# A gated linear attention and a four-expert block on one core: the last two groups of tokens share each expert's weights, and the attention state is stored in 96 columns

## The chip, the cores and the metric

The kernel runs on one core of a Trainium2 chip. The metric is the device time of one launch in microseconds; the kernel before the change takes 1087.85 us (median of 3 runs, 1086.94 to 1088.24). The engines are named as the profile names them: PE is the matrix engine (PEld its weight loads), DVE the vector engine, ACT the scalar engine, POOL the general engine, SP the engine that issues most of the transfers.

## What is computed

A recurrent attention with a decay for each key dimension comes first. Its output, 3072 tokens of 384 features, goes through four experts of two layers each, whose results are added with normalized weights.

```python
# B, H, S, D = 4, 8, 768, 48
for t in range(S):
    state = alpha[:, :, t, :, None] * state + einsum('bhd,bhe->bhde', k[:, :, t], v[:, :, t])
    y[:, :, t] = einsum('bhd,bhde->bhe', q[:, :, t], state)
x = y.transpose(0, 2, 1, 3).reshape(3072, 384)
# E, F = 4, 1024
p = domain_probs / (domain_probs.sum(-1, keepdims=True) + 1e-09)
for e in range(E):
    out += p[:, e:e + 1] * (maximum(x @ w1[e], 0.0) @ w2[e])
```

All data are float32.

## The kernel before

**Units and groups.** The sequence is cut into 6 blocks of 128 steps; a block of one batch is a *unit*, so there are 24. Attention makes 128 tokens of x from a unit. The experts work on groups of units: group 0 has 2, groups 1 to 5 have 4 each (512 tokens), and group 6, the last, has 2 (256 tokens). A group goes through all four experts before the next begins, with an `up` (first layer) and a `down` (second layer) for each.

**Two ways to multiply.** A float32 product is either done *whole*, [...] (two matmul records in the trace), or *in parts*: both factors are split into parts that fit the faster `float32r` type, and three matmuls give the product. Splitting the weights is done once, in groups 0 and 1, and the parts are kept in DRAM; splitting x and the hidden activations costs work on ACT and DVE.

```python
split1 = lambda gi, e, c=0: gi > 0 and (gi < len(groups) - 1 or c < NQ - 1)   # first layer
split2 = lambda gi, e, c=0: 1 < gi < len(groups) - 1                          # second layer
```

So before the change group 6 runs its first layer in parts for three of the four weight pieces (a piece is a quarter of F, two of the eight `fc` tiles), and the fourth piece and its whole second layer as whole float32.

**The first layer**, for one tile `fc` of 128 hidden features (PSUM tiles with the tag "g" come from a ring of four):

```python
one = ps.tile([P, NT], F32, name="one", tag="g", bufs=4)[:, :hi - lo]
...
two = ps.tile([P, NT], F32, name="two", tag="g", bufs=4)[:, :n]
for out, terms in ((one, (1, 0)), (two, (2,))):
    for part in terms:
        for kc in range(KC):
            nc.tensor.matmul(out, lhsT=w[:, part, kc], rhs=xTs[gi][:, part, kc, :n], ...)
while finish:                       # the rest of the tile before
    for _ in finish.popleft(): pass
t = work.tile([P, NT], F32, name="t")[:, :n]
nc.scalar.activation(out=t, in_=one, func=ACT.Copy, scale=FINE)
if split2(gi, e):
    nc.vector.tensor_add(t, t, two)
    finish.append(hidden_parts(t, parts))
else:
    nc.vector.tensor_add(whole, t, two)
    finish.append(rectified(whole))
...
def hidden_parts(x, parts):
    top, low, dif = parts
    nc.scalar.activation(out=top, in_=x, func=ACT.Relu, scale=TRIM)
    yield
    nc.vector.scalar_tensor_tensor(out=low, in0=x, scalar=0.0, in1=top.bitcast(F32),
                                   op0=ALU.max, op1=ALU.subtract)
    n = x.shape[-1]
    make_dif(*(part[:, :n // 2] for part in parts))      # one more DVE operation, half the columns
    later.append([part[:, n // 2:] for part in parts])   # the other half, done during down
```

**The second layer** takes two units at a time where it is in parts (four PSUM tiles), one unit at a time where it is whole (one PSUM tile). Each result is added into the accumulator of its unit:

```python
nc.vector.scalar_tensor_tensor(out=acc, in0=part, scalar=scale, in1=acc,
                               op0=ALU.mult, op1=ALU.add)
```

**Attention** runs in the background. Each unit is a generator of 17 steps (`BEATS`); `deal()` gives every step a moment on a clock that counts the matmuls of the experts, and `advance()` emits the steps that are due between those matmuls. Two units are under way at a time. The x of a group is finished before the second layer of the last expert of the group before, where `split_x` splits it. The parts of a unit that the change touches:

```python
st = sts[b]                                      # [P, NP=4, 2, HD=64]: two heads of a pair, 64 columns each
yps = ps.tile([P, KC, P], F32, name="yps", tag="w")
for c in range(KC):                              # KC = 3
    if c < 2:
        turns = [[(j, 2 * c + j // 2, j % 2, slice(0, QUAD)) for j in range(4)]]      # QUAD = 32
    else:
        turns = [[(p, p, i, slice(QUAD, HD)) for p in range(NP)] for i in range(2)]
    terms = [(t, past) for past in ((True, False) if cb > 0 else (False,)) for t in turns]
    for n, (turn, past) in enumerate(terms):
        for j, p, i, cols in turn:
            nc.tensor.matmul(yps[QUAD * j:QUAD * (j + 1), c, :],
                             lhsT=st[:, p, i, cols] if past else rv[:, 2 * p + i, cols],
                             rhs=QT[:, p, :] if past else lat[:, 2 * p + i, :], ...)
...
sps = ps.tile([P, NP, 2, HD], F32, name="sps", tag="w")
for p in range(NP):                              # 128 x 128 products, the new part of the state
    nc.tensor.matmul(sps[:, p], lhsT=KB[:, p, :], rhs=rv[:, 2 * p:2 * p + 2, :], start=True, stop=True)
```

`past` is what the state of the earlier blocks adds; the 20 units with cb > 0 have it.

Of the kernel before, what the change touches and what calls it, by code (L numbers as in the profile page):

```python
# [20 lines left out]
def kernel(  # L21
# [41 lines left out]
    P = 128  # L63
# [40 lines left out]
    lat = const.tile([P, H, P], F32, name="lat")  # L104
    sts = [const.tile([P, NP, 2, HD], F32, name=f"st{b}") for b in range(B)]

# [3 lines left out]
    half = B // 2  # L110
    groups = [order[:half]] + [order[i:i + B] for i in range(half, len(order), B)]
    units = [u for g in groups for u in g]
    place = {u: (gi, i) for gi, g in enumerate(groups) for i, u in enumerate(g)}
# [33 lines left out]


    split1 = lambda gi, e, c=0: gi > 0 and (gi < len(groups) - 1 or c < NQ - 1)
    split2 = lambda gi, e, c=0: 1 < gi < len(groups) - 1  # L150
    makes = [lambda gi, e: gi == 0, lambda gi, e: gi == 1]


    def load(u, names):
        if u >= len(units):
            return
        cb, b = units[u]
        for nm in names:
            src = srcs[nm][b, :, cb * P:(cb + 1) * P, :].rearrange("h s d -> s h d")
            if nm != "v":  # L160
                nc.sync.dma_start(out=raw(u, nm)[:, :, :D], in_=src)
                continue

            pairs = raw(u, nm).rearrange("p (a i) d -> p a i d", i=2)
            src = src.rearrange("p (a i) d -> p a i d", i=2)
            nc.sync.dma_start(out=pairs[:, :, 0, :D], in_=src[:, :, 0])
            nc.sync.dma_start(out=pairs[:, :, 1, :QUAD], in_=src[:, :, 1, :QUAD])
            nc.sync.dma_start(out=pairs[:, :, 1, D:], in_=src[:, :, 1, QUAD:])

# [3 lines left out]
            for l in range(2)]  # L173
    wt = ({}, {})

    AHEAD = 4
# [4 lines left out]
    def load_piece(l, i, beside=False):  # L181
        if i >= E * NQ * len(groups):
            return
        gi, k = divmod(i, E * NQ)
        e, c = divmod(k, NQ)
        if (split1, split2)[l](gi, e, c):
            w = wt[l][i] = wts.tile([P, 3, KC * QF], F32R, name=f"w{l + 1}",
                                    bufs=AHEAD if l == 0 else NQ)
            nc.sync.dma_start(out=w.bitcast(F32), in_=kept[l][k])
            return  # L190
# [72 lines left out]
    def attention(u):  # L263
# [139 lines left out]

        st = sts[b]
        yps = ps.tile([P, KC, P], F32, name="yps", tag="w")
        for c in range(KC):

            if c < 2:
                turns = [[(j, 2 * c + j // 2, j % 2, slice(0, QUAD)) for j in range(4)]]
            else:  # L410
                turns = [[(p, p, i, slice(QUAD, HD)) for p in range(NP)] for i in range(2)]
            terms = [(t, past) for past in ((True, False) if cb > 0 else (False,)) for t in turns]
            for n, (turn, past) in enumerate(terms):
                for j, p, i, cols in turn:
                    nc.tensor.matmul(  # L415
                        yps[QUAD * j:QUAD * (j + 1), c, :],
                        lhsT=st[:, p, i, cols] if past else rv[:, 2 * p + i, cols],
                        rhs=QT[:, p, :] if past else lat[:, 2 * p + i, :],
                        start=(n == 0), stop=(n == len(terms) - 1))
        gi, slot = place[cb, b]  # L420
        if slot == 0:
            if gi == 0:
                xTs[gi] = work.tile([P, 3, KC, NT], F32R, name="xT", bufs=1)
                xraws[gi] = xTs[gi][:, 2].bitcast(F32)
            else:
                xraws[gi] = work.tile([P, KC, NT], F32, name="x_raw", bufs=1)
        nc.scalar.copy(out=xraws[gi][:, :, slot * P:(slot + 1) * P], in_=yps)
        yield

        if cb < NCB - 1:  # L430
            KB = AT
            nc.scalar.copy(out=KB, in_=turned(lambda p: KT[:, p, :]))
            yield
            sps = ps.tile([P, NP, 2, HD], F32, name="sps", tag="w")
            for p in range(NP):
                nc.tensor.matmul(sps[:, p], lhsT=KB[:, p, :], rhs=rv[:, 2 * p:2 * p + 2, :],  # L436
                                 start=True, stop=True)
            for i in range(2):
                rows = slice(HD * i, HD * (i + 1))
                old, add = st[rows, :, i, :], sps[rows, :, i, :]  # L440
                if cb == 0:
                    nc.vector.tensor_copy(out=old, in_=add)
                else:
                    nc.vector.tensor_mul(old, old, decs[-1][rows].broadcast_to([HD, NP, HD]))
                    nc.vector.tensor_add(old, old, add)

        load(u + 2, "v")
        yield

    def split_x(gi, step):  # L450

        n = len(groups[gi]) * P
        if step == 0:
            xTs[gi] = work.tile([P, 3, KC, NT], F32R, name="xT", bufs=1)
            for kc in range(KC):
                nc.scalar.activation(out=xTs[gi][:, 0, kc, :n], in_=xraws[gi][:, kc, :n],
                                     func=ACT.Copy, scale=TRIM)
        else:
            kc = step - 1
            split_rest(xraws[gi][:, kc, :n], [xTs[gi][:, part, kc, :n] for part in range(3)])  # L460


    def up(gi, e, fc, slots=None):
# [3 lines left out]
        c, f = divmod(fc, FPQ)  # L467
        i = (gi * E + e) * NQ + c
        if fc == 0 and begins:
# [12 lines left out]
        col = slice(f * P, (f + 1) * P)  # L482
        if split1(gi, e, c):
            w = wt[0][i].rearrange("p t (c f) -> p t c f", f=QF)[:, :, :, col]
# [4 lines left out]
        one = ps.tile([P, NT], F32, name="one", tag="g", bufs=4)[:, :hi - lo]  # L489
        if not split1(gi, e, c):  # L490
            for kc in range(KC):
# [3 lines left out]
        else:  # L495
            two = ps.tile([P, NT], F32, name="two", tag="g", bufs=4)[:, :n]
            for out, terms in ((one, (1, 0)), (two, (2,))):
                for part in terms:
                    for kc in range(KC):
                        nc.tensor.matmul(out, lhsT=w[:, part, kc], rhs=xTs[gi][:, part, kc, :n],  # L500
                                         start=(part == terms[0] and kc == 0),
# [16 lines left out]
        if f == FPQ - 1 and ends:  # L518
            if gi > 0:
                del wt[0][i]  # L520
                load_piece(0, i + AHEAD)
            elif i == E * NQ - 1:
                for k in range(AHEAD):
                    load_piece(0, i + 1 + k)
            while late:
# [23 lines left out]
    def down(gi, e, slots, between):  # L549


        first = (gi * E + e) * NQ
        halves_ = split2(gi, e)
# [32 lines left out]
        background()  # L586
        if slots[-1] == len(groups[gi]) - 1:
            while makes[1](gi, e) and (making or splitting):
                background()

            for c in range(NQ):
                del wt[1][first + c]
                if c < NQ // 2:
                    load_piece(1, first + NQ + c)
# [3 lines left out]
    def add_up(gi, e, slot, kind, part):  # L598
# [3 lines left out]
        if e == 0 and (kind == 0 or not split2(gi, e)):  # L602
            accs[cb, b] = hid.tile([P, DM], F32, name="acc", bufs=B)
        acc = accs[cb, b]
# [8 lines left out]
        if e == E - 1:  # L613
            del accs[cb, b]
            row = b * S + cb * P
            stores.append(lambda: (nc.sync if gi == len(groups) - 1 else nc.gpsimd).dma_start(
                out=out[row:row + P, :], in_=acc))
# [9 lines left out]
    def deal():  # L627
# [6 lines left out]
        t = 0.0  # L634
        for gi in range(len(groups)):
            for e in range(E):
                part = 1 - 1 / len(groups[0]) if gi == e == 0 else 1
                t += cost(0, gi, e) * FCH * part
                if e == E - 1:
                    wanted.append(t)  # L640
                t += cost(1, gi, e) * len(groups[gi]) * part
        for gi in range(1, len(groups)):
            n = len(groups[gi])
            first = wanted[gi - 1] if gi > 1 else 0.0
            space = (wanted[gi] - MARGIN - first) / (n if gi > 1 else (n + 1) / 2)
            if gi == 1:
                space /= 2
            for k in range(n):
                u = sum(map(len, groups[:gi])) + k
                end = wanted[gi] - MARGIN - (n - 1 - k) * space  # L650
                begin = max(end - 2 * space, ends[-2])
# [11 lines left out]
    with tc.manual_schedule():  # L663
# [47 lines left out]

        for gi, e in ((gi, e) for gi in range(len(groups)) for e in range(E)):
            rest = gi == e == 0
# [5 lines left out]
            for k, slots in enumerate(turns):  # L719

                between = deque()
                if e == E - 1 and gi + 1 < len(groups):
                    for step, at in enumerate((0.0, 0.52, 0.62, 0.72)):
                        at = at * len(turns) - k
                        if 0 <= at < 1:
                            between.append((at, lambda step=step: split_x(gi + 1, step)))
                down(gi, e, slots, between)
                if gi == len(groups) - 1 and e == E - 1:
                    stores.popleft()()
        while stores:  # L730
# [29 lines left out]
```

## Time and profile before

| | from the page or the trace |
|---|---|
| time | 1087.85 us (profiled execution: span 1085.3 us) |
| busy share of PE, DVE, ACT, POOL | 98%, 69%, 52%, 3% |
| clock granted to PE | full but for short spells (0.998 in the mean) |
| chain that ended last | PE 87%, ACT 5%, DVE 5% |
| up and down of one expert of group 4, with attention between | 696.8 to 719.3 us and 719.3 to 739.3 us |
| up and down of the last expert of group 5, no attention left | 970.9 to 987.4 us and 987.4 to 1004.4 us |
| group 6, from its first matmul to the last | 1004.4 to 1081.7 us |
| transfers | 273.68 MB, 252 GB/s in the mean |

The page gives busy time of each engine, the span in 40 slices, the chain of work that ended last, and groups of instructions with the mean duration of one. [...] the pace of a row of matmuls is read from start to start in the timeline, not from that mean. A line in the timeline merges neighbours of one kind: start, length, engine, line, and how many.

### The profile page before, as it was taken

The page shows a single profiled execution, that of the slowest core. Times are in us where ns is not written, and L with a number is a line of the kernel's source. Part 1 is how long each engine was busy: PE and PEld are TensorE (multiplying, and loading weights), DVE is VectorE, ACT ScalarE, POOL GpSimd, SP SyncE. Part 2 cuts the span into 40 slices and gives each one's busy share as a digit, 9 for nine tenths or more (in the row PEclk, how much of TensorE's full clock was granted, in tenths as well). Part 3 has the DMA queues.
Part 4 walks back from the last instruction along what each step waited for, and adds up shares of the span by engine and source line. Part 5 has one row for each costly group of instructions (what it writes and reads, how often), then busy time and mean ns, then how long its engine had stood idle before and what let it go on. Part 6 is the DMA issues. An engine that isn't in the chain of part 4 may idle for free.

```text
span 1085.3 us, 21700 instructions
## 1 busy us (share of the span) xinstructions
PE 1062.9 (98%) x8532; PEld 892.9 (82%) x8532; DVE 747.7 (69%) x1625; ACT 560.7 (52%) x1191; POOL 35.3 (3%) x75
## 2 busy tenths in 40 slices
PE   8889899999999999999999999999999999999998
PEld 8767677686776798898898898898988998899876
DVE  5588678647557869778878787986786876757111
ACT  5787776674646555545546445555454454222321
POOL 2000000000000100000000000000000000000000
PEclk9999999999999999999999999999999999999999
DMA  8597789786696967657759559477477568545982
GB/s 124 154 327 216 228 266 370 290 312 234 211 322 218 400 203 275 273 169 301 254 171 358 201 190 357 158 276 306 151 291 287 201 259 349 235 197 238 309 312 91
DMA packets 166197, 273.68 MB, mean 252 GB/s; under 512 B 120624, under 2 KB 140976, under 8 KB 142032
## 3 DMA queue, kind: packets, MB, share of 16 engines
q1 hardware_dynamic: 156704, 230.06, 61.0%
q0 software_dynamic: 6016, 42.08, 9.9%
q8 instruction: 67, 1.10, 0.4%
q10 hardware_dynamic: 3376, 0.17, 0.3%
q14 instruction: 34, 0.28, 0.1%
HBM read 229.81 MB, written 42.47 MB: 251 GB/s over the span
## 4 chain that ended last, share of the span: by engine, by line
PE 87%; ACT 5%; DVE 5%; issue 2%; POOL 0%; ACTq 0%; DVEq 0%; POOLq 0%
PE ops L576 24%; PE one L500 21%; PE ops L580 13%; PE two L500 10%; PE sc L328 6%; PE yps L415 4%; PE one L492 3%; PE tp L260 3%; ACT qb L302 2%; PE sps L436 1%; PE far L383 1%; PE idle L689 1%; DVE near L338 1%; DVE hT L534 1%; DVE t L509 1%
## 5 line engine op out<-in xcount | busy, mean ns | idle before, releaser
L576 PE MATMUL ops<-w,hT 128*128 128x384 f32 x1536 | 284.7, 340 | 2.1 <-DVE acc L609 2.1
L500 PE MATMUL one<-xT,w 128*128 128x512 f32 (+1 forms) x1104 | 275.3, 385 | 0.8 <-DVE xT L242 0.8
L576 PEld LDWEIGHTS ops<-w,hT 128*128 128x128 f32 x1536 | 265.9, 188 | 5.7 <-DVE acc L609 2.8
L500 PEld LDWEIGHTS one<-xT,w 128*128 128x128 f32 x1104 | 194.5, 188 | 43.4 <-issue 2.6
L507 ACT ACTIVATE t<-one 128x512 f32<-128x512 f32 (+1 forms) x184 | 103.1, 560 | 149.4 <-PE one L500 148.8
L580 PE MATMUL ops<-hT 128*128 128x384 f32 x512 | 176.1, 491 | 0.0
L302 ACT COPY qb<-QT 64x256 f32<-64x256 f32 x336 | 136.5, 406 | 70.1 <-DVE QT L283 40.2
L500 PE MATMUL two<-xT,w 128*128 128x512 f32 (+1 forms) x552 | 148.3, 377 | 0.0
L580 PEld LDWEIGHTS ops<-hT 128*128 128x128 f32 x512 | 94.0, 191 | 56.5 <-issue 1.3
L534 DVE SCALAR_TENSOR_TENSOR hT<-t,hT 128x512 fp32r<-128x512 f32 x128 | 88.7, 693 | 61.1 <-ACT hT L532 59.7
L532 ACT ACTIVATE hT<-t 128x512 fp32r<-128x512 f32 x128 | 80.9, 632 | 95.8 <-DVE t L509 94.6
L500 PEld LDWEIGHTS two<-xT,w 128*128 128x128 f32 x552 | 100.3, 188 | 19.8
L542 DVE SCALAR_TENSOR_TENSOR hT<-hT 128x256 fp32r<-128x256 f32 x256 | 101.3, 421 | 4.4
L509 DVE TENSOR_TENSOR t<-t,two 128x512 f32<-128x512 f32 x128 | 87.3, 682 | 20.6 <-PE two L500 12.6
L609 DVE SCALAR_TENSOR_TENSOR acc<-ops,p_all,acc 128x384 f32<-128x384 f32 x88 | 53.3, 612 | 58.6 <-PE ops L580 42.3
L338 DVE COPY_PREDICATED near<-masks,sc 128x256 f32<-128x256 uint8 x144 | 77.0, 535 | 17.6 <-PE sc L328 14.5
L309 DVE TENSOR_TENSOR QT<-QT,dec 128x256 f32<-128x256 f32 x144 | 60.7, 421 | 32.5 <-ACT qb L302 32.0
L328 PEld LDWEIGHTS sc<-qb,KT 128*64 128x64 f32 x2304 | 72.5, 138 | 8.9 <-issue 6.3
L512 DVE TENSOR_TENSOR hT<-t,two 128x512 f32<-128x512 f32 (+1 forms) x56 | 32.1, 574 | 65.8 <-ACT t L507 56.1
L328 PE MATMUL sc<-qb,KT 128*64 128x64 f32 x2304 | 76.7, 223 | 0.3 <-ACT qb L302 0.3
L321 DVE TENSOR_TENSOR KT<-KT,dec 128x256 f32<-128x256 f32 x144 | 60.1, 417 | 2.2 <-PE tp L260 2.2
L320 ACT COPY KT<-KT 128x256 f32<-128x256 f32 x144 | 59.8, 415 | 3.1
(79 smaller groups left out, 927.0 us busy)
## 6 DMA issues: line engine op xcount, KB each, us to landing
w<-kept SPq DMA_DIRECT2D x156, 1152.0 KB
kept<-w POOLq DMA_DIRECT2D x32, 1152.0 KB, 7.5
hT<-in_moe_w_dram SPq DMA_DIRECT2D x48, 384.0 KB
w<-in_moe_w_dram SPq DMA_DIRECT2D x60, 128.0 KB
ra<-in_alpha_dram SPq DMA_DIRECT2D x23, 192.0 KB
rk<-in_k_dram SPq DMA_DIRECT2D x23, 192.0 KB
rq<-in_q_dram SPq DMA_DIRECT2D x23, 192.0 KB
out_dram<-acc POOLq DMA_DIRECT2D x22, 192.0 KB, 5.8
```

The costliest lines, as they stand in the source:

```text
L302: nc.scalar.copy(out=qb[rows, :, i, :].rearrange("p a (b r) -> p a b r", r=m), in_=qv[rows])
L309: nc.vector.tensor_mul(qv, qv, spread(dv[:, :, :, 0], m))
L328: nc.tensor.matmul(out[HALF * s:HALF * (s + 1), 2 * p:2 * p + 2, :], lhsT=KTs[li][:, p, HALF * s:HALF * (s + 1)], rhs=qbs[li][:, p, :, QUA ...
L338: nc.vector.copy_predicated(near.rearrange("p a (b two r) -> p a b two r", two=2, r=m)[:, :, :, 1, :], mk.unsqueeze(1).broadcast_to([P, H, ...
L500: nc.tensor.matmul(out, lhsT=w[:, part, kc], rhs=xTs[gi][:, part, kc, :n], start=(part == terms[0] and kc == 0), stop=(part == terms[-1] a ...
L507: nc.scalar.activation(out=t, in_=one, func=ACT.Copy, scale=FINE)
L509: nc.vector.tensor_add(t, t, two)
L532: nc.scalar.activation(out=top, in_=x, func=ACT.Relu, scale=TRIM)
L534: nc.vector.scalar_tensor_tensor(out=low, in0=x, scalar=0.0, in1=top.bitcast(F32), op0=ALU.max, op1=ALU.subtract)
L542: nc.vector.scalar_tensor_tensor(out=dif, in0=top.bitcast(F32), scalar=1 / 4096.0, in1=low.bitcast(F32), op0=ALU.mult, op1=ALU.subtract)
L576: nc.tensor.matmul(sums[i][part // 2], lhsT=h[:, part], rhs=w, start=(fc == 0 and part != 1), stop=(fc == FCH - 1 and part != 0))
L580: nc.tensor.matmul(sums[i][0], lhsT=h[:, 2].bitcast(F32), rhs=w, start=(fc == 0), stop=(fc == FCH - 1))
```

## The change

It has four parts.

1. **Group order.** Groups 0 to 4 are worked as before. The last two groups are then worked side by side: expert 0 on group 5, expert 0 on group 6, expert 1 on group 5, and so on. Group 6 uses the weight pieces that group 5 loaded, and the next expert's pieces are loaded as group 6 lets go of them.
2. **Group 6 in parts.** Both of its layers are now in parts throughout. Its split x lies in five tiles that attention has finished with, its unsplit x in two others, its accumulators in the QT tiles.
3. **Pace.** Group 6's x is now wanted after group 5's first `up`. The six attention units of groups 5 and 6 are therefore dealt at one even pace, over group 4 and the beginning of group 5; before, group 5's four were spread over group 4 and group 6's two over group 5.
4. **State in 96 columns.** A pair of heads now lies in 2 x 48 columns with no gap: first head, then the last 16 features of the second, then its first 32. The 16 left-over features of both heads are thereby neighbours, and one matmul per pair covers both in the `past` term of c = 2. The sps product has 96 moving columns in place of 128, and the update of the state on DVE 192 elements in place of 256 per partition.

The core of the diff, with cuts marked by "...":

```diff
-    sts = [const.tile([P, NP, 2, HD], F32, name=f"st{b}") for b in range(B)]
+    sts = [const.tile([P, NP, 2, D], F32, name=f"st{b}") for b in range(B)]
...
+    LAST = len(groups) - 1
+    tasks = [(gi, e) for gi in range(LAST - 1) for e in range(E)]
+    tasks += [(gi, e) for e in range(E) for gi in (LAST - 1, LAST)]
...
-    split1 = lambda gi, e, c=0: gi > 0 and (gi < len(groups) - 1 or c < NQ - 1)
-    split2 = lambda gi, e, c=0: 1 < gi < len(groups) - 1
+    split1 = lambda gi, e: gi > 0
+    split2 = lambda gi, e: gi > 1
...
-            nc.sync.dma_start(out=pairs[:, :, 1, :QUAD], in_=src[:, :, 1, :QUAD])
-            nc.sync.dma_start(out=pairs[:, :, 1, D:], in_=src[:, :, 1, QUAD:])
+            nc.sync.dma_start(out=pairs[:, :, 1, :TAIL], in_=src[:, :, 1, QUAD:])
+            nc.sync.dma_start(out=pairs[:, :, 1, TAIL:D], in_=src[:, :, 1, :QUAD])
...
+    first_piece = lambda gi, e: (min(gi, LAST - 1) * E + e) * NQ
...
+                now = [[(2 * c + j // 2, j % 2, (0, HD + TAIL)[j % 2], 2 * QUAD * (j % 2))
+                        for j in range(4)]]
+                turns = ([(True, now[0])] if cb > 0 else []) + [(False, now[0])]
             else:
-                turns = [[(p, p, i, slice(QUAD, HD)) for p in range(NP)] for i in range(2)]
+                turns = [(True, [(p, 0, 0, QUAD) for p in range(NP)])] if cb > 0 else []
+                turns += [(False, [(p, i, QUAD + TAIL * i, 0) for p in range(NP)]) for i in range(2)]
...
-                nc.tensor.matmul(sps[:, p], lhsT=KB[:, p, :], rhs=rv[:, 2 * p:2 * p + 2, :],
+                nc.tensor.matmul(sps[:, p], lhsT=KB[:, p, :], rhs=rv[:, 2 * p:2 * p + 2, :D],
...
-            if gi > 0:
+            elif gi != LAST - 1:
                 del wt[0][i]
                 load_piece(0, i + AHEAD)
...
-                if c < NQ // 2:
+                if c < NQ // 2 or gi == LAST:
                     load_piece(1, first + NQ + c)
...
+            accs[cb, b] = hid.tile([P, DM], F32, name="acc", bufs=B) if gi < LAST else \
+                work.tile([P, NP * P], F32, name="QT")[:, :DM]
...
-        for gi in range(1, len(groups)):
-            n = len(groups[gi])
+        for gis in [*([gi] for gi in range(1, LAST - 1)), [LAST - 1, LAST]]:
+            gi, due = gis[0], wanted[gis[-1]] - MARGIN
+            n = sum(len(groups[i]) for i in gis)
...
-        for gi, e in ((gi, e) for gi in range(len(groups)) for e in range(E)):
+        for (gi, e), after in zip(tasks, [*tasks[1:], (None, None)]):
```

## Prediction, made before the changed kernel was run

> **What bounds the kernel now.** I began with the page: the busy shares, then the 40 slices.
>
> ```profile
> PE 1062.9 (98%) x8532; PEld 892.9 (82%) x8532; DVE 747.7 (69%) x1625; ACT 560.7 (52%) x1191; POOL 35.3 (3%) x75
> PE   8889899999999999999999999999999999999998
> DVE  5588678647557869778878787986786876757111
> ```
>
> PE is busy throughout, and DVE only 10% busy in the last three slices, which are group 6. [...] I checked with the waits: from 380 us on, PE and its weight loads wait less than 10 us in all, and the only long ones are two of some 1.2 us, on DVE (`acc`), at 515 and 685 us, when the x of the next group is split. Every attention product there runs at one fixed length, 1.88 us for `yps` for instance, however DVE stands. So PE's own work sets the time nearly everywhere: a matmul taken away is worth its pace, unless its removal lets another engine come last.
>
> The windows say how much room the others have, here the last down of group 3, then an up and a down of group 4 (columns: PE, PEld, DVE, ACT, POOL busy; clock; DMA share; GB/s).
>
> ```profile
> 675.60:696.80 21.20, 20.19 (x153) 19.25 (x148) 19.50 (x46) 9.11 (x20) 1.08 (x2) 1.00 0.35 98
> 739.30:761.50 22.20, 22.20 (x214) 18.30 (x214) 17.64 (x38) 13.84 (x28) 0.00 (x0) 1.00 0.94 378
> 761.50:781.30 19.80, 19.80 (x149) 19.38 (x148) 16.32 (x42) 8.12 (x20) 0.00 (x0) 1.00 0.36 95
> ```
>
> DVE is 79 to 82% busy in an ordinary up and down, 92% where x is split.
>
> **Group 6 in parts: the matmuls.** One expert of group 6 in PE's timeline (start, length, engine, line, count):
>
> ```profile
> 1047.37 0.87 PE L500 MATMUL one<-xT,w 128*128 128x256 f32 x6
> 1048.43 0.87 PE L500 MATMUL one<-xT,w 128*128 128x256 f32 x6
> 1049.49 2.75 PE L492 MATMUL one<-x_raw,w 128*128 128x256 f32 x12
> 1052.08 10.48 PE L580 MATMUL ops<-hT 128*128 128x384 f32 x32
> 1062.10 1.14 PE L500 MATMUL one<-xT,w 128*128 128x256 f32 x6
> ```
>
> From start to start: a tile in parts takes 1048.43 - 1047.37 = 1.06 us (nine matmuls at 0.1175), the two whole tiles 1052.08 - 1049.49 = 2.59 us, the whole down of both units 1062.10 - 1052.08 = 10.02 us. The whole expert is 19.27 us (1042.83 to 1062.10). In parts: up 8 x 1.06 = 8.5 us; down 2 units x 8 tiles x 3 matmuls = 48 at 0.174 us (the 96 of a down of group 5, 987.4 to 1004.4 us, go at this pace) = 8.35 us. Together 16.85: **2.4 us less an expert, 9.7 us in all**, if nothing else comes last.
>
> **Group 6 in parts: what comes last.** In parts, a tile of hidden features has a chain on ACT and DVE. An up of group 5 without attention shows it:
>
> ```profile
> 978.16 0.68 DVE L509 TENSOR_TENSOR t<-t,two 128x512 f32<-128x512 f32 x1
> 978.88 0.63 ACT L532 ACTIVATE hT<-t 128x512 fp32r<-128x512 f32 x1 [1.33 <-DVE t L509]
> 979.41 0.58 ACT L507 ACTIVATE t<-one 128x512 f32<-128x512 f32 x1
> 979.54 0.69 DVE L534 SCALAR_TENSOR_TENSOR hT<-t,hT 128x512 fp32r<-128x512 f32 x1 [0.70 <-ACT hT L532]
> 980.27 0.42 DVE L542 SCALAR_TENSOR_TENSOR hT<-hT 128x256 fp32r<-128x256 f32 x1
> 980.61 0.68 DVE L509 TENSOR_TENSOR t<-t,two 128x512 f32<-128x512 f32 x1
> ```
>
> The sum `t` of one tile is followed by its relu, then `low`, then half of `dif`, and only then by the next tile's sum: 0.72 + 0.66 + 0.73 + 0.34 = 2.45 us a tile, while PE needs 2.06. It is a chain and not a load: DVE stands idle 0.70 us in it, waiting for the relu, and cannot go on to the next sum, which stands behind in program order. [...] With 512 columns this lag stays hidden: 8 x 0.39 = 3.1 us of it just fit into the ring of four PSUM tiles and into the first matmuls of down, which don't need the last tiles.
>
> With 256 columns PE takes half the time, but the chain doesn't, because each operation has a fixed part: 512 columns take 0.68, 256 take 0.42, so 128 take about 0.28 (estimated on the same line). The four steps become 0.45 + 0.45 + 0.46 + 0.20 = **1.56 us a tile against 1.06**. I followed the ring of four by hand, from the start of up: the first sum can start at 1.33 us (as in group 6 now), the k-th at 1.33 + 1.56 k; `two` of tile k+2 needs sum k to have ended, `one` of tile k+2 needs the copy `t` of tile k, which ends 1.14 us after sum k-1 starts. PE meets this first at tile 5 (0.49 us late), then at 6 and 7 (0.5 us each): up ends at 9.96 instead of 8.46 us, and the first matmul of down waits another 0.37 us for the copy of tile 6. That is **1.9 us lost an expert, 7.5 us in all**, and leaves 0.5 us an expert, about 2 us, of the 9.7. Now the chain in group 6 is only sum and relu, 1.18 us a tile, which PE hardly feels.
>
> **State in 96 columns.** The `yps` of one unit, the part c = 2:
>
> ```profile
> 748.54 0.62 PE L415 MATMUL yps<-QT,st 128*32 128x128 f32 x16
> 748.98 0.62 PE L415 MATMUL yps<-lat,rv 128*32 128x128 f32 x16
> 749.53 0.74 PE L500 MATMUL one<-xT,w 128*128 128x512 f32 x2
> ```
>
> The 16 records of the past take 748.98 - 748.54 = 0.44 us; 8 of them go, 0.22 us, in 20 units: **4.4 us, all on PE's path**. [...] four records share one 0.109 us stretch, so the gain is 8/4 stretches and not eight matmuls.
>
> The `sps` product is different.
>
> ```profile
> 758.52 1.05 PE L436 MATMUL sps<-rv,AT 128*128 128x128 f32 x8
> 758.29 1.09 PEld L436 LDWEIGHTS sps<-rv,AT 128*128 128x128 f32 x8
> ```
>
> A matmul here starts every 0.11 us, and its weights, 128 columns, load just as fast. [...] where a load of 128 columns is exposed in this trace the next follows after 0.11 us as well. So the load will set the pace of 96 columns too, and I count next to nothing, 0.3 us (if only the stream counted, it would be a quarter of 0.81 us in 20 units: 4 us). The shorter update of the state saves DVE about 0.3 us a unit, not on the path.
>
> **Pace.** On the dealing clock an expert of four units is 8 x 2.1 + 4 x 4.1 = 33.2 us. Group 4 saw one unit per expert; now the six units share one group plus one expert less 6 us, 160 us, so 26.6 us each. Attention takes PE about 42.0 - 33.2 = 9 us and DVE some 13 us a unit, so DVE's load in group 4 goes from some 80% to some 86%. In an up the heaviest case I see is 14 us for the eight chains' own work plus 9 or 10 of attention, part of it in the idle 0.70 us of each tile, in 22 to 23 us of PE: just about enough. I put 1.0 us on it, and another 1.2 us because the end of group 4, where x is split, now has full attention beside it, as groups 2 and 3 have in the two waits at 515 and 685 us. Group 5 loses its attention, which cost no waits.
>
> **Transfers.** Twelve fewer pieces from DRAM and fewer raw ones, some 22 MB. The next expert's first-layer pieces may start only as group 6's up lets go of them: the first has about 15 us until group 5 wants it, and a piece (1.18 MB) needs 3 us at the 380 to 400 GB/s of the busy windows. The four second-layer pieces have the 16.5 us of an up for 12 us. I expect no wait.
>
> **Sum.** 1087.85 - 2.2 (group 6) - 4.4 (yps) - 0.3 (sps) + 1.0 + 1.2 = 1083.2; I shade it to **1082.5 us**, as both the lag and the load limit of sps would err downwards.
>
> **Rivals.** (a) PE alone counts: the ring hides the lag, and sps follows its columns: 1087.85 - 9.7 - 4.4 - 4 = 1070. For it: PE was the bound nearly everywhere. Against it: the 1.56 against 1.06 us. (b) The second is that attention at the tighter pace becomes DVE-bound and PE waits for `lat` or for PSUM in group 4, 2 us an expert: 1087 to 1090. For it: the 92% window. Against: not one attention product waited since 170 us. (c) The third is that the weights arrive late, since no piece is loaded a whole group ahead any more; 2 to 3 us an expert would end above 1088. Against: the arithmetic above.
>
> **Range and chances.** Half of (a) gives about 1075, half of (b) about 1087. Over 2% faster is under 1066.1, beyond even (a): 3%. Over 2% slower needs over 1109.6: 2%.
>
> **What would show it.** Right: group 6's ups last about 10.3 us from first `one` to first `ops`, not 8.5, with PE idle or its weight loads waiting on the ACT copy `t` and the DVE sum; sums in its ups 1.56 us apart; its down 8.35 us; `yps` 1.66 instead of 1.88 us; sps still at 0.8 us for eight; DVE over 85% in group 4. Wrong: ups of 8.5 us (the lag isn't there), sps at 0.65 us, several waits of attention products in group 4, or `w` behind a DMA in group 5.

## The result, and the profile after

The changed kernel takes **1084.63 us** (median of 4 runs, 1083.29 to 1085.53) against 1087.41 us for the kernel before (4 runs), a ratio of 0.9973 with a 95% interval of 0.9955 to 0.9990. It is faster by 2.8 us, 0.3% (by the interval, 1.1 to 4.9 us); the prediction said 1082.5 us in a range of about 1075 to 1087.

The lines of the page that answer to those shown of before, and below them the chain that ended last (before, PE 87%, ACT 5%, DVE 5%):

```profile
PE 1058.0 (98%) x8460; PEld 899.7 (83%) x8460; DVE 779.0 (72%) x1743; ACT 564.3 (52%) x1202; POOL 32.8 (3%) x71
PE   8889899999999999999999999999999999999998
DVE  5578678647557869778878777986787965756565
PE 78%; DVE 10%; ACT 8%; issue 3%; DMA 1%; SPq 0%; ACTq 0%; DVEq 0%
```

PE's busy time is 4.9 us shorter and its row the same. What is new shows in the chain: DVE and ACT now hold 18% of it. DVE's row has 5 to 7 tenths where group 6 used to leave it at 1.

The chain of the changed kernel in one `up` of group 6, in order of time (start, length, what), tells why:

```profile
959.15 0.42 DVE t L540
959.58 0.02 issue
959.60 0.42 ACT hT L563
960.03 0.02 issue
960.05 0.44 DVE hT L565
960.49 0.02 issue
960.51 0.04 DVE hT L573
960.55 0.17 issue
960.72 0.42 DVE t L540
```

From one sum (`t` L540) to the next there are 960.72 - 959.15 = 1.57 us, through relu, `low` and the start of `dif`; not one matmul lies on this stretch. PE's timeline beside it keeps the same beat:

```profile
960.34 0.98 PE L531 MATMUL one<-KT,w 128*128 128x256 f32 x6
...
961.91 0.97 PE L531 MATMUL one<-KT,w 128*128 128x256 f32 x6
```

1.57 us from `one` to `one`, where PE's own nine matmuls take 1.08, as in the first tiles of an `up`. Still PE is hardly ever shown idle: from 960 to 980 us it counts as busy for 19.58 of 20 us. The six `one` of a tile last 0.97 or 0.98 us here and 0.88 us in the first tiles of the same `up`, so that longer records fill most of the gap. Weight loads waiting for the copy `t` show 3.8 us of it in group 6.

The difference of the two profiled executions (1085.3 and 1083.0 us), stretch by stretch:

| stretch | before, us | after, us | difference |
|---|---|---|---|
| up to group 4 | 696.85 | 694.60 | -2.25 |
| groups 4 and 5 (after: without the three finished experts of group 6 between) | 307.55 | 308.24 | +0.7 |
| group 6 to the end | 80.9 | 80.16 | -0.7 |

What is gained lies ahead of group 4, where of the four parts of the change only the state in 96 columns is at work; the rework of the last groups about cancels itself. The experiments take this apart.

### The profile page after: what moved, and what is told of

Its sections match the earlier page's. It is cut to its first block, busy times and chain, and to the rows that moved or that the text cites. A ratio compares the mean times of both kernels' runs of the same rounds, so it can differ in the third digit from the quotient of the medians.

```text
span 1083.0 us, 21627 instructions
## 1 busy us (share of the span) xinstructions
PE 1058.0 (98%) x8460; PEld 899.7 (83%) x8460; DVE 779.0 (72%) x1743; ACT 564.3 (52%) x1202; POOL 32.8 (3%) x71
## 4 chain that ended last, share of the span: by engine, by line
PE 78%; DVE 10%; ACT 8%; issue 3%; DMA 1%; SPq 0%; ACTq 0%; DVEq 0%
PE ops L607 25%; PE one L531 19%; PE two L531 9%; PE ops L611 9%; PE sc L333 5%; PE yps L425 3%; PE tp L265 3%; ACT qb L307 2%; DVE t L540 2%; PE one L523 2%; DVE hT L565 2%; ACT hT L563 2%; PE sps L454 1%; DVE near L343 1%; PE far L388 1%
## 5 line engine op out<-in xcount | busy, mean ns | idle before, releaser
L607 PE MATMUL ops<-w,hT 128*128 128x384 f32 x1728 | 318.1, 340 | 1.9 <-DVE acc L641 1.4
L607 PEld LDWEIGHTS ops<-w,hT 128*128 128x128 f32 x1728 | 299.2, 188 | 6.9 <-DVE acc L641 2.7
L531 PE MATMUL one<-xT,w 128*128 128x512 f32 x960 | 254.1, 400 | 0.8 <-DMA w<-kept 0.4
L563 ACT ACTIVATE hT<-t 128x512 fp32r<-128x512 f32 (+1 forms) x160 | 94.3, 589 | 122.1 <-DVE t L540 120.8
L565 DVE SCALAR_TENSOR_TENSOR hT<-t,hT 128x512 fp32r<-128x512 f32 (+1 forms) x160 | 102.1, 638 | 75.4 <-ACT hT L563 74.1
L531 PE MATMUL two<-xT,w 128*128 128x512 f32 x480 | 136.4, 393 | 0.0
L611 PE MATMUL ops<-hT 128*128 128x384 f32 x384 | 135.3, 496 | 0.0
L573 DVE SCALAR_TENSOR_TENSOR hT<-hT 128x256 fp32r<-128x256 f32 (+1 forms) x320 | 117.3, 394 | 5.5
L540 DVE TENSOR_TENSOR t<-t,two 128x512 f32<-128x512 f32 (+1 forms) x160 | 100.5, 628 | 23.7 <-PE two L531 14.8
L531 PEld LDWEIGHTS two<-xT,w 128*128 128x128 f32 x480 | 90.2, 188 | 19.9
L611 PEld LDWEIGHTS ops<-hT 128*128 128x128 f32 x384 | 70.0, 192 | 40.5 <-issue 1.6
```

Source lines behind the costliest of these rows:

```text
L531: nc.tensor.matmul(out, lhsT=w[:, part, kc], rhs=x_part(gi, part, kc), start=(part == terms[0] and kc == 0), stop=(part == terms[-1] and k ...
L573: nc.vector.scalar_tensor_tensor(out=dif, in0=top.bitcast(F32), scalar=1 / 4096.0, in1=low.bitcast(F32), op0=ALU.mult, op1=ALU.subtract)
L607: nc.tensor.matmul(sums[i][part // 2], lhsT=h[:, part], rhs=w, start=(fc == 0 and part != 1), stop=(fc == FCH - 1 and part != 0))
L611: nc.tensor.matmul(sums[i][0], lhsT=h[:, 2].bitcast(F32), rhs=w, start=(fc == 0), stop=(fc == FCH - 1))
```

## The experiments

All were timed against the kernel before; ratios are to it, with 95% intervals. An `up` is counted from its first `one` to the first `ops`, a `down` from there to the next `one`. The stretches are those of one profiled execution each, the times are medians.

### The 96 columns alone

On the kernel before, only the state in 96 columns:

```diff
-    sts = [const.tile([P, NP, 2, HD], F32, name=f"st{b}") for b in range(B)]
+    sts = [const.tile([P, NP, 2, D], F32, name=f"st{b}") for b in range(B)]
     # and the loads of v, the turns of yps, sps[..., :D] and the update of the state, as in the change
```

> The kernel before with nothing changed but the state in 96 columns (loads of v, yps, sps, state update). Main theory: only the yps matmuls of the past count, 8 of 64 records, 0.22 us a unit in 20 units, 4.4 us less than before, near 1083.0 us; yps at 1.67 us a unit, the eight sps records still in 0.81 us. Rival: sps follows its columns and gives 4 us more, near 1079 us, with sps at about 0.65 us.

Measured: 1084.0 us, ratio 0.9962 (0.9948 to 0.9975). A unit's `yps` went from 1.884 to 1.666 us, which in 20 units is 4.4 us; the eight `sps` records kept their 0.807 us (from 327 us on). So this part alone gives what the whole change gives: **the other three parts together bring nothing** that these runs resolve (1084.63 against 1084.0).

### The order of the operations in group 6

In the changed kernel, for group 6 only, the copy and the sum of a tile are emitted ahead of the relu, `low` and `dif` of the tile before. Nothing is added or taken away.

```diff
-            while finish:
+            first = gi == LAST
+            while finish and not first:
                 for _ in finish.popleft():
                     pass
             t = work.tile([P, NT], F32, name="t")[:, :n]
             nc.scalar.activation(out=t, in_=one, func=ACT.Copy, scale=FINE)
             ... the sum, without the two finish.append that stood there ...
+            while finish:
+                for _ in finish.popleft():
+                    pass
+            finish.append(hidden_parts(t, parts) if split2(gi, e) else rectified(whole))
```

> The changed kernel, with one thing moved in group 6 alone: the copy t and the sum of tile fc are emitted ahead of the relu, low and dif of tile fc-1, so that no sum stands behind a relu in the queue of DVE. Main theory (the chain sum, relu, low, dif, sum of 1.57 us a tile holds PE back through the ring of four PSUM tiles): ups of group 6 fall from 10.4 us to about 8.6 us, 1.8 us an expert, 7 us in all, near 1077.5 us. Rival 1 (the weight loads of 256-column matmuls or the arrival of the weights hold the ups back): unchanged, 1084.6 us. Rival 2 (DVE is short of time, not of order): ups stay above 9.5 us, gain under 3 us.

Measured: 1076.98 us, ratio 0.9898 (0.9882 to 0.9915). The second `up` of group 6, first in the changed kernel, then in this run:

```profile
954.62 0.88 PE L531 MATMUL one<-KT,w 128*128 128x256 f32 x6
965.04 0.79 PE L607 MATMUL ops<-w,hT 128*128 128x384 f32 x3
```

```profile
953.73 0.87 PE L531 MATMUL one<-KT,w 128*128 128x256 f32 x6
962.50 0.79 PE L610 MATMUL ops<-w,hT 128*128 128x384 f32 x3
```

All four ups of group 6 take 8.77 or 8.78 us here; in the changed kernel three took 10.4 us and one 10.7. That is 6.9 of the 7.7 us that went. The pages count the same instructions on every engine (8460 on PE, 1743 on DVE, 1202 on ACT), so the cause is the order, not DVE's load and not the weights.

### A longer chain

The changed kernel, with all of group 6's `dif` made in the up:

```diff
         n = x.shape[-1]
+        if n == 2 * P:
+            make_dif(*parts)
+            return
         make_dif(*(part[:, :n // 2] for part in parts))
```

> The changed kernel, with dif of group 6 made whole in the up (256 columns) instead of half there and half in the down; DVE has no more elements to do in all. Main theory: the chain of a tile grows from 1.57 to 1.71 us, five such steps stand before the last tile of an up, so ups of group 6 go from 10.4 to 11.0 or 11.1 us, 0.65 us an expert, 2.6 us in all, near 1087.2 us. Rival (something other than the chain sets the ups): 1084.6 us or a little less, as an operation of 128 columns has more fixed cost than half of one of 256.

Measured: 1086.84 us, ratio 0.9994 (0.9986 to 1.0002), 2.2 us above the changed kernel. Three of its ups of group 6 take 11.08 us, 0.67 us more than the 10.41, and the fourth 11.37 in place of 10.71; five tiles, each with a chain longer by 0.13 or 0.14 us (in the changed kernel `dif` takes 0.42 us with 256 columns and 0.29 with 128), were expected to give 0.65. Made longer, the chain costs PE what it grows; taken out, it gives that back.

### The sum first in all groups in parts

The same order for groups 2 to 6, with a third buffer for `t`:

```diff
-            first = gi == LAST
+            first = split2(gi, e)
...
-            t = work.tile([P, NT], F32, name="t")[:, :n]
+            t = work.tile([P, NT], F32, name="t", bufs=3)[:, :n]
```

> As the run with the sum first in group 6, but in every group whose second layer is in parts (groups 2 to 6), with a third buffer for t. Main theory: the lag of some 3 us that an up of 512 columns builds up costs PE only some 0.2 to 0.3 us at the beginning of each down, so 16 ups give 3 to 5 us more than the run with group 6 alone, near 1074 us. Rival: with 512 columns the lag is hidden by the ring and by the first matmuls of down, and nothing more comes of it, near 1077.5 us.

Measured: **1071.73 us**, ratio 0.9839 (0.9822 to 0.9857): 5.2 us less than with group 6 alone. This version beats both kernels. The third buffer was not run without the new order, and attention takes buffers of `t` too (for `own`), so the 5.2 us belong to the two together. DVE's timeline in an up of group 6:

```profile
954.03 0.42 DVE L541 TENSOR_TENSOR t<-t,two 128x256 f32<-128x256 f32 x1
954.37 0.42 DVE L568 SCALAR_TENSOR_TENSOR hT<-t,hT 128x256 fp32r<-128x256 f32 x1
954.82 0.29 DVE L576 SCALAR_TENSOR_TENSOR hT<-hT 128x128 fp32r<-128x128 f32 x1
955.11 0.42 DVE L541 TENSOR_TENSOR t<-t,two 128x256 f32<-128x256 f32 x1
```

The same three operations now repeat every 1.08 us, with no wait for a relu between them. The chain that ended last reads

```profile
PE 89%; ACT 4%; DMA 2%; DVE 2%; issue 1%; SPq 0%; ACTq 0%; DVEq 0%
```

Where an `up` of 512 columns has nothing special beside it, the lag of 3 us was hidden, as predicted: the first three experts of group 2 take 125.8 us in this run and in the one with group 6 alone. Groups 2 to 4 are 4.9 us shorter all the same, in other places. The last downs of groups 2 and 3, where x is split, went from 21.0 us to some 19.9; their two waits for `acc` on DVE, 1.4 us together, are gone. Group 4 went from 172.6 to 170.3 us, 1.05 us of it in its long `yps` (below), from 2.73 to 1.68 us. The 0.2 to 0.3 us at the beginning of each down, from which the expectation made its 3 to 5 us, are not there: its total was met in other places, which is luck.

### Group 1 as well

```diff
-            first = split2(gi, e)
+            first = True
```

> The changed kernel with the sum first in all groups 2 to 6, and in group 1 as well, where the second layer is whole and the chain is only sum and relu. Theory: group 1 runs its ups at PE's pace already (its second layer is so long that nothing is behind), so within 1 us of 1071.7. Rival: the copy t behind the relu holds its ups back too, 2 us or more less.

Measured: 1070.8 us, ratio 0.9843 (0.9830 to 0.9857), not to be told from the run before it. Group 1's second layer is whole and its chain only sum and relu; the new order gives it nothing that this measurement resolves.

### The new order without the new grouping

The kernel before with 96 columns (the first experiment) and the sum first in groups 2 to 5:

```diff
-            while finish:
+            first = split2(gi, e)
+            while finish and not first:
                 for _ in finish.popleft():
                     pass
     # and the rest as above; group 6 stays alone and half whole
```

> The kernel before with the state in 96 columns and the sum first in groups 2 to 5, group 6 as it was (alone, half whole). With the sum first in all groups the changed kernel went from 1077.0 to 1071.7 us over the run with group 6 alone, so the same 5 us should come here: near 1078.8 us. If so, group 6 in parts and side by side is worth the 7 us between this and 1071.7 once the chain is out of the way: 9.7 us of matmuls less 1.5 to 2 us for the tight pace. Rival (the order matters only together with the new grouping): near 1083 us.

Measured: 1078.79 us, ratio 0.9917 (0.9903 to 0.9930). Together with the others this makes a square (96 columns in all four, the third buffer for `t` in the right column):

| | relu first | sum first |
|---|---|---|
| group 6 after group 5, half whole | 1084.0 us | 1078.8 us |
| group 6 side by side, in parts | 1084.6 us | 1071.7 us |

The regrouping is worth 7.1 us, if nothing stands in its way, and nothing that shows where the chain does. In the two traces of the right column, group 6 takes 72.1 us to the end in place of 80.7, and groups 4 and 5 take 305.2 us in both: the 1.5 to 2 us that the expectation took off for the tight pace are not there.

### In parts, but not side by side

Group 6 in parts after group 5, with its own loads and the old pace:

```diff
-    tasks = [(gi, e) for gi in range(LAST - 1) for e in range(E)]
-    tasks += [(gi, e) for e in range(E) for gi in (LAST - 1, LAST)]
+    tasks = [(gi, e) for gi in range(LAST + 1) for e in range(E)]
...
-    first_piece = lambda gi, e: (min(gi, LAST - 1) * E + e) * NQ
+    first_piece = lambda gi, e: (gi * E + e) * NQ
...
-        for gis in [*([gi] for gi in range(1, LAST - 1)), [LAST - 1, LAST]]:
+        for gis in ([gi] for gi in range(1, LAST + 1)):
```

> The changed kernel with group 6 in parts in both layers, but after group 5 and with weights loaded for itself, and with the old pace of attention (each group over the group before). Main theory: an expert of group 6 needs 9.4 MB of weight parts, 24 us at the 390 GB/s of the busy windows, against 19 us of PE, so group 6 is bound by its transfers, 4 to 6 us an expert, 15 to 22 us in all less the 3 us that the tight pace costs: near 1098 us, with weight loads of PE waiting for DMA. Group 4 without its waits for lat. Rival: loading ahead hides the transfers, and the time is that of the changed kernel less the cost of the pace, near 1082 us.

Measured: 1100.25 us, ratio 1.0108 (1.0090 to 1.0125). Three of the downs of group 6 take 12.9 to 16.1 us and the last 9.9, in place of 8.5, and PE waits for the weights there (waits from 1000 us on: who, for whom, us in total, times, longest):

```profile
PEld ops L606 <- DMA w<-kept: 12.2, 4, 5.1
PE ops L606 <- DMA w<-kept: 10.9, 4, 4.8
```

So this is what sharing the weights is for: without it the two layers in parts cost 16 us against the 96 columns alone, which has the same order of groups and the same pace, where with it they cost nothing that shows. In the changed kernel PE waits for `w<-kept` 0.4 us in the whole execution. (The waits don't fill the whole 16 us by which the three downs are longer than the changed kernel's. The clock granted to PE was 0.87, 0.79 and 0.87 in them; if PE's time grows as that clock falls, which no run shows by itself, 8.5 us become 9.8, 10.8 and 9.8, by estimate another 4.9 us, which with the 10 or 11 us of waits in these three makes up most of the 16. Why the clock fell was not tried.)

### A tighter pace

The 96 columns alone, with group 5's four units dealt at half the space, in the last half of group 4. Group 6's two units had to begin later for it, after group 5's.

```diff
-            if gi == 1:
+            if gi in (1, len(groups) - 2):
                 space /= 2
...
                 begin = max(end - 2 * space, ends[-2])
+                if gi == len(groups) - 1:
+                    begin = ends[-1] if k == 0 else (ends[-2] + ends[-1]) / 2
```

> The kernel before with the state in 96 columns, and with the four attention units of group 5 dealt at 16 us on the clock instead of 33, in the last half of group 4 (the changed kernel has 26.6). DVE's load there is some 20 us x 16/33 + 13 = 23 us in 25 us of PE. Theory: the cost of a tight pace grows steeply from the 1.5 us seen at 26.6: 3 to 8 us more than the 1084.0 of the 96 columns alone, with yps waiting for lat and far for qb. Rival: PE stays the bound and it costs under 1.5 us.

Measured: 1088.64 us, ratio 1.0006 (0.9997 to 1.0014), 4.6 us above the 96 columns alone. `far`, `yps`, `qb` and `lat` are products and tiles of attention. The waits in that stretch include

```profile
PEld far L383 <- ACT qb L302: 4.9, 2, 3.7
PE far L383 <- DVE t L279: 3.4, 1, 3.4
```

neither of which stands in the kernel before from 690 us on. It was `far` that waited; the expected wait of `yps` for `lat` did not come. At 26.6 on the clock, in the changed kernel, the cost is smaller and of the same kind: groups 4 and 5 take 308.2 us, against 306.9 in the 96 columns alone. With the sum first it is gone, 305.2 against 305.2 (above), so at 26.6 it comes with the old order or with two buffers for `t`, and not with DVE's load alone. Its longest wait is in PE's timeline in group 4:

```profile
803.24 0.43 PE L425 MATMUL yps<-QT,st 128*32 128x128 f32 x8
804.51 0.43 PE L425 MATMUL yps<-lat,rv 128*32 128x128 f32 x8 [0.85 <-ACT lat L405]
```

### The sps product at 48 columns

The second head of each pair is left out of the update of the state (it takes the first head's columns instead), so this is another computation, run once for its trace:

```diff
-                nc.tensor.matmul(sps[:, p], lhsT=KB[:, p, :], rhs=rv[:, 2 * p:2 * p + 2, :D],
+                nc.tensor.matmul(sps[:, p, 0], lhsT=KB[:, p, :], rhs=rv[:, 2 * p, :D],
...
-                old, add = st[rows, :, i, :], sps[rows, :, i, :]
+                old, add = st[rows, :, i, :], sps[rows, :, 0, :]
```

> The changed kernel, with the sps product cut to 48 moving columns: the update of the state for the second head of each pair is left out (it takes the first head's columns), so the output differs. Theory: the load of 128 weight columns sets the pace, and the eight sps records keep their 0.81 us, 0.11 us from start to start, as with 128 and with 96 columns. Rival: [...] the stream counts at last: under 0.7 us for eight.

Measured: the first line is the changed kernel, with the one that follows it there, the next two are this run.

```profile
458.10 1.02 PE L454 MATMUL sps<-rv,AT 128*128 128x96 f32 x8
458.90 0.95 PE L531 MATMUL one<-xT,w 128*128 128x512 f32 x3
```

```profile
457.14 0.98 PE L454 MATMUL sps<-rv,AT 128*128 128x48 f32 x8
457.95 1.41 PE L531 MATMUL one<-xT,w 128*128 128x512 f32 x5
```

The records overlap (those of `sps` in the first line last 0.24 to 0.28 us each), so their starts are compared. From first `sps` to the next product there are 0.80 and 0.81 us: 128, 96 and 48 columns take the same. From start to start the seven steps are 108, 110, 112, 111, 112, 112, 111 ns with 128 columns, 81, 110, 112, 112, 111, 112, 112 with 96 and 42, 110, 112, 111, 112, 112, 111 with 48. Only the first step follows the columns, and what it saves is lost again at the end: from the last `sps` to the product behind it there are 31, 57 and 97 ns. The six other steps stay at 0.11 us, and so do those of the weight loads beside them. A fixed cost of 0.11 us for every float32 record is not what does it: `sc`, an attention product with 64 columns of weights and 64 moving columns, goes two side by side in steps of 0.058 us. The time of this single run, 1083.44 us, is not used.

## Why the prediction was right, point by point

**PE as the bound, and where it stops being it.** Right, and the result hung on it. Counting matmuls alone (the first rival) would have said 1070 us. The chain was read off an up with 512 columns and scaled to 256: 1.56 us a tile predicted, 1.57 measured, with the steps 0.45, 0.45, 0.46 and 0.21 us where 0.45, 0.45, 0.46 and 0.20 were written down. The fixed part of a DVE operation was the term that mattered: a sum takes 0.68 us with 512 columns in both traces, and the sums of this chain, with 256, take 0.41 to 0.42 us; by estimate from these two, about 0.15 us don't shrink with the columns. The operation with 128 columns is not a sum but `dif`: 0.28 us was the estimate from the trace before (the line through 0.68 and 0.42 gives 0.29), and the trace after has 0.29. That the lag stays hidden at 512 columns was right for an ordinary `up` and wrong where x is split.

**Group 6.** The lag was right, the sum too good. Predicted were an up of 10.3 us and a down of 8.35; measured 10.4 (one of 10.7) and 8.5 to 8.6. An expert takes 18.9 to 19.3 us instead of 19.2 or 19.3 before, so group 6 gave 0.7 us and not 2.2. Of the 1.5 us between, some 0.7 lie in the downs, some 0.6 in the ups (0.3 of it in the long one) and 0.2 in the time from the last matmul to the end. The pace of 0.1175 us a matmul was too good as well, which counts once the lag is gone: an up still takes 8.62 us in the run with the sum first in all groups, where 72 matmuls at 0.1175 would take 8.46, so 0.1197 us each. (For comparison, from start to start a whole product's record with 256 columns takes 0.216 us in the trace before, and such a product has two: 0.43 us against three in parts at 0.1175, 0.35 us.) The matmuls in parts read x from other tiles than before; what makes them 2% slower was not tried.

**yps and sps.** 4.4 us predicted, 20 x 0.218 = 4.4 in the trace and 4.1 in the time. For sps 0.3 was counted and nothing came; the steps after the first stay at 0.11 us, as do those of the weight loads, down to 48 columns. That the loads set the pace was the author's estimate; the runs don't show which of the two holds the other.

**Pace.** 2.2 us predicted, 1.3 measured against the 96 columns alone. The total was near, the place wrong in part: the 1.2 us put on the split of x at the end of group 4 did not come (that down takes 19.2 us, against 20.0 in the 96 columns alone), while `yps` and `far` did wait in group 4, which 1.0 us had been put on; such waits stood in the prediction as a sign of being wrong. Another sign failed: DVE is 81% busy in group 4 (139.97 of 172.40 us; 78% before), not over 85. The prediction's own figures, 13 us a unit beside some 21 us of an expert's chains, give some 84% and not 86.

**Transfers.** No wait was predicted and 0.4 us measured, and the run without sharing shows that this wasn't to be taken for granted. The third rival is out; the second, DVE-bound attention, is right in kind and too large in size at this pace. It comes at a tighter one, with 4.6 us.

**The total.** The forecast gain was 5.4 us and 2.8 came, so that the total is less good than the chain. Group 6 gave 1.5 us less than predicted and the pace cost 0.9 us less; that the two errors cancel in part is luck. The step from 1083.2 to 1082.5 us went the wrong way: the ups came out at 10.4 us for 10.3, and sps gave nothing.

## What to carry to other kernels

Before counting on fewer matmuls, write down the chain that one tile runs through on the other engines, from one pass of the loop to the next in each engine's own order, and compare it with PE's time for a tile: a chain that hides at 512 columns may not at 256, since an operation on half the columns takes well over half the time (0.42 against 0.68 us here). If it is longer, look at the order first: emit the operation that frees PSUM ahead of the rest of the tile before, and the chain becomes a load, which here turned a regrouping that brought nothing into one worth 7 us, and the whole change into 1.6%. And don't count a small matmul by its columns alone: `sps` kept 0.81 us for eight from 128 moving columns down to 48, in step with the loads of its 128 weight columns.

## What the runs showed that was not expected

- The sum first, with a third buffer, was worth 5.2 us in the groups of 512 columns too. It did not come in their ordinary ups and downs, where the lag is hidden, but where other work stands beside the chain: at the split of x, where the list of waits had shown it before, and in group 4 at its tight pace.
- A step of `sps` follows the columns once, right after a product with long streams (81 ns for 96, 42 ns for 48), and then never again. That the second load had been done ahead, behind that stream, is not what the trace records: in all three runs it starts 1 or 2 ns after the first `sps`. The cause stays open.
